# Windowed attention followed by a highway layer: x transposed by a DMA, and the set-up moved off VectorE

## The chip, the cores and the metric

The kernel runs on one core of a Trainium2 chip. The metric is the time of one execution on the device, in microseconds (us). Each kernel was run several times; a run counts as fast when it lies within 1.5% of the fastest run of the same kernel, and only fast runs are compared. Ratios are the mean time of one kernel's fast runs over that of the other kernel's fast runs of the same rounds, so they are not quite the ratio of the medians that are quoted. Spans (139.0, 159.3) are those of the one profiled execution, from its first to its last instruction, and are a little shorter than the run's time. The granted clock is the share of full speed at which the chip let TensorE run.

## The reference, cut to what matters

```python
batch, n_heads, seq, head_dim = (4, 8, 768, 64)
n_sink, window = (4, 128)
scores = scale * np.matmul(q, k.transpose(0, 1, 3, 2))
keep = is_sink | in_window          # the first 4 keys, and the last 128
a = softmax(where(keep, scores, -1e9))
attn = np.matmul(a, v)
x = attn.transpose(0, 2, 1, 3).reshape(B * S, H * D)      # 3072 x 512
H = np.maximum(x @ w_h, 0.0)
T = 1.0 / (1.0 + np.exp(-(x @ w_t + b_t)))
out = T * H + (1.0 - T) * x
```

## The kernel before

The 3072 tokens are worked through in 24 chunks of 128 tokens (six chunks per batch). One trip of the loop holds pieces of four chunks, so that the engines overlap. The two products of the highway layer contract over the 512 features of x, and the program's matmuls for them read x with its features on the partitions: x, called `xh` in the program, is transposed into `xT` between the attention of a chunk and its highway layer. What TensorE computes is then copied (evacuated) by ScalarE or VectorE into the tile that the next step reads.

```python
    def stage_T(n):                       # q and k of a chunk: transposed on TensorE
        ...
        nc.scalar.copy(out=qT, in_=tp[:, 0:NHP, :])
        nc.vector.tensor_copy(out=kT, in_=tp[:, NHP:2 * NHP, :])

    def stage_sink_setup(b):              # once per batch: the 4 sink keys and values
        for hh in range(2):
            nc.vector.tensor_copy(out=ks3[rows, :, 4 * hh:4 * hh + NSINK],
                                  in_=kT[rows, :, 0:NSINK])
        ...  # two TensorE matmuls with a selection matrix into vps, then
        for g in range(2):
            nc.vector.tensor_tensor(out=vs[:, g, :, :], in0=vps..., in1=bdm..., op=ALU.mult)

    def stage_A(n):                       # weights times v, then the division
        ...
        nc.vector.reciprocal(out=rec.unsqueeze(2), in_=avh[:, :, 64:65])
        nc.vector.tensor_tensor(out=xh, in0=avh[:, :, 0:D], in1=rec..., op=ALU.mult)

    def stage_X(n):                       # x transposed on TensorE
        for j in range(NOC):
            nc.tensor.transpose(xtp[:, j, :], xh[:, 2 * j:2 * j + 2, :], ident)
        nc.scalar.copy(out=xT, in_=xtp)

    def stage_Mt(n):                      # the gate: x @ w_t into tps, tanh
    def stage_Mh(n):                      # x @ w_h into hps, then dd, ee, otok on VectorE
        ...
        nc.sync.dma_start(out=out[n * P:(n + 1) * P, :], in_=otok)

        for i in range(-2, NB + 1):
            s = i + 1
            ...                           # sink scores of i and i+1, every second trip
            stage_S(s); stage_A(i); stage_T(i + 2)
            load(i + 2 + AHEAD); load_v(i + 2 + AHEAD)      # AHEAD = 8 chunks
            stage_mask(s); stage_Mt(i - 1); stage_X(i)
            stage_sink_setup(i // NSC)    # in the first chunk of a batch
            stage_Mh(i - 1)
```

`xT` of chunk i is made in trip i and used in trip i+1, by `stage_Mt(i)`. The loads of q, k and v are issued by GpSimd and come in pieces of 256 bytes of input (one head of one token, 64 numbers), cast to fp16 on the way; the trace records each load of 128 tokens as 1024 packets of 128 bytes. The stores are issued on the sync engine's queue.

The softmax here doesn't subtract the row's maximum and nothing guards it: scores larger than these inputs give would overflow.

Of the kernel before, what the change touches and what calls it, by code (L numbers as in the profile page):

```python
# [8 lines left out]

FP16 = mybir.dt.float16  # L10
FP32 = mybir.dt.float32
# [10 lines left out]
def kernel(  # L22
# [19 lines left out]
    P = 128  # L42
# [49 lines left out]
        nc.gpsimd.dma_start(out=vt[:, :, 0:D], in_=v[b, :, rows, :].transpose([1, 0, 2]))  # L92


    ebias = const.tile([P, 1], FP32, tag="ebias")
    nc.vector.memset(ebias, _EXP_BIAS)
    wh_sb = const.tile([P, NOC, DM], FP16, tag="wh")
    wt_sb = const.tile([P, NOC, DM], FP16, tag="wt")
    ident = const.tile([P, P], FP16, tag="ident")
    mask = const.tile([P, 2, P], FP16, tag="mask", name="mask")  # L100
    nc.vector.memset(ident, 1.0)
    nc.vector.memset(mask, 1.0)
    for vt in v_ring:
        nc.vector.memset(vt, 2.0)

    with tc.manual_schedule(engines={ENG.Pool}):
        load(0)
        nc.gpsimd.affine_select(
            out=ident, in_=ident, compare_op=ALU.is_equal, fill=0.0,
            base=0, pattern=[[-1, P]], channel_multiplier=1)  # L110
        load_v(0)
        load(1)

        nc.gpsimd.affine_select(
            out=mask[:, 1, :], in_=mask[:, 1, :], compare_op=ALU.is_ge, fill=0.0,
            base=0, pattern=[[1, P]], channel_multiplier=-1)
        load_v(1)
        nc.gpsimd.affine_select(
            out=mask[:, 0, :], in_=mask[:, 0, :], compare_op=ALU.is_ge, fill=0.0,
            base=-1, pattern=[[-1, P]], channel_multiplier=1)  # L120
        load(2)
        nc.gpsimd.dma_start(out=wt_sb, in_=moe_w_t.rearrange("(kc p) of -> p kc of", p=P))
        load_v(2)
        load(3)
        nc.gpsimd.dma_start(out=wh_sb, in_=moe_w_h.rearrange("(kc p) of -> p kc of", p=P))
        load_v(3)
        bdm = const.tile([P, H], FP32, tag="bdm")
        nc.gpsimd.memset(bdm, 1.0)
        bdm3 = bdm.rearrange("p (a b) -> p a b", b=2)
        nc.gpsimd.affine_select(  # L130
            out=bdm3, in_=bdm3, compare_op=ALU.is_ge, fill=0.0,
            base=0, pattern=[[-32, NHP], [-4, 2]], channel_multiplier=1)
        nc.gpsimd.affine_select(
            out=bdm3, in_=bdm3, compare_op=ALU.is_ge, fill=0.0,
            base=NSINK - 1, pattern=[[32, NHP], [4, 2]], channel_multiplier=-1)
        for n in range(4, AHEAD):
            load(n)
            load_v(n)

    mask0 = const.tile([P, P], FP16, tag="mask0", name="mask0")  # L140
    nc.vector.tensor_copy(out=mask0, in_=mask[:, 1, :])
    nc.vector.memset(mask0[0:NSINK, :], 1.0)
    mask1 = const.tile([P, 2, P], FP16, tag="mask1", name="mask1")
    nc.vector.tensor_copy(out=mask1, in_=mask)
    nc.vector.memset(mask1[0:NSINK, 0, :], 1.0)


    bt32 = const.tile([1, DM], FP32, tag="bt32")
# [3 lines left out]
    ones_row = const.tile([P, P], FP16, tag="ones_row")  # L152
    nc.vector.memset(ones_row, 0.0)
    nc.vector.memset(ones_row[0:1, :], 1.0)
    nc.vector.tensor_scalar_mul(bt16[0:1, :], bt32, 0.5)


    sel = const.tile([P, NHP, 32], FP16, tag="sel")
    nc.vector.memset(sel, 0.0)
    for hh in range(2):  # L160
        nc.vector.tensor_copy(
            out=sel[:, :, 4 * hh:4 * hh + NSINK],
            in_=ident[:, 0:NSINK].unsqueeze(1).to_broadcast([P, NHP, NSINK]))
    ks_bd = []
    for i in range(2):
        t = const.tile([P, NHP * 160], FP16, tag=f"ks{i}", name=f"ks{i}")
        nc.vector.memset(t, 0.0)
        ks_bd.append(t)


    qkT = {}
    e_of = {}
    es_of = {}
    vs_of = {}
    xh_of = {}
    xT_of = {}

    def stage_T(n):
        qsd, ksd = qk_sd.pop(n)
        tp = m_ps.tile([P, 2 * NHP, P], FP16, tag="m", name="tp")  # L180
        for j in range(NHP):
            nc.tensor.transpose(tp[:, j, :], qsd[:, 2 * j:2 * j + 2, :], ident)  # L182
        for j in range(NHP):
            nc.tensor.transpose(tp[:, NHP + j, :], ksd[:, 2 * j:2 * j + 2, :], ident)  # L184
        qT = qkT_pool.tile([P, NHP, P], FP16, tag="qT", name="qT")
        kT = qkT_pool.tile([P, NHP, P], FP16, tag="kT", name="kT")
        nc.scalar.copy(out=qT, in_=tp[:, 0:NHP, :])  # L187
        nc.vector.tensor_copy(out=kT, in_=tp[:, NHP:2 * NHP, :])  # L188
        qkT[n] = (qT, kT)

    def stage_sink_setup(b):

        _, kT = qkT[b * NSC]
        ks = ks_bd[b % 2]
        ks3 = ks.rearrange("p (a b) -> p a b", b=160)
        for hh in range(2):
            rows = slice(64 * hh, 64 * hh + 64)
            nc.vector.tensor_copy(out=ks3[rows, :, 4 * hh:4 * hh + NSINK],
                                  in_=kT[rows, :, 0:NSINK])
        vps = av_ps.tile([P, 2, 512], FP32, tag="av", name="vps")  # L200
        vt = v_ring[(b * NSC) % NV]
        for g in range(2):
            nc.tensor.matmul(vps[:, g, 0:260], lhsT=sel.rearrange("p a b -> p (a b)"),
                             rhs=vt[:, g * 260:(g + 1) * 260], start=True, stop=True)
        vs = es_pool.tile([P, 2, 4, 65], FP16, tag="vs", name="vs")
        for g in range(2):
            nc.vector.tensor_tensor(  # L207
                out=vs[:, g, :, :],
                in0=vps[:, g, 0:260].rearrange("p (h e) -> p h e", e=65),
                in1=bdm[:, 4 * g:4 * g + 4].unsqueeze(2).to_broadcast([P, 4, 65]),  # L210
                op=ALU.mult)
        vs_of[b] = vs

    def stage_sink(n):

# [46 lines left out]
    def stage_A(n):  # L262
        b, c = divmod(n, NSC)
        es, np_ = e_of.pop(n)
        vts = ([] if c == 0 else [v_ring[(n - 1) % NV]]) + [v_ring[n % NV]]
        av = av_ps.tile([P, 2, 4, P], FP32, tag="av", name="av")
        for g in range(2):
            first = True
            for hl in range(2):
                for hh in range(2):  # L270
                    h = 2 * (2 * g + hl) + hh
                    for pc, vt in enumerate(vts):
                        nc.tensor.matmul(  # L273
                            av[:, g, 2 * hl + hh, 0:_AVN], lhsT=es[g][:, hh, hl, pc, :],
                            rhs=vt[:, 65 * h:65 * h + _AVN], start=first,
                            stop=False, skip_group_check=True)
                        first = False
            if c >= 2:
                nc.tensor.matmul(
                    av[:, g, :, 0:65], lhsT=es_of[n][:, c % 2, :],  # L280
                    rhs=vs_of[b][:, g, :, :], start=False, stop=True,
                    skip_group_check=True)
        es_of.pop(n, None)
        avh = av.rearrange("p g h e -> p (g h) e")
        rec = r_pool.tile([P, H], FP32, tag="rec", name="rec")
        nc.vector.reciprocal(out=rec.unsqueeze(2), in_=avh[:, :, 64:65])
        xh = x_pool.tile([P, H, D], FP16, tag="xh", name="xh")
        nc.vector.tensor_tensor(  # L288
            out=xh, in0=avh[:, :, 0:D],
            in1=rec.unsqueeze(2).to_broadcast([P, H, D]), op=ALU.mult)  # L290
        xh_of[n] = xh

    def stage_X(n):
        xh = xh_of[n]
        xtp = av_ps.tile([P, NOC, P], FP16, tag="av", name="xtp")
        for j in range(NOC):
            nc.tensor.transpose(xtp[:, j, :], xh[:, 2 * j:2 * j + 2, :], ident)  # L297
        xT = x_pool.tile([P, NOC, P], FP16, tag="xT", name="xT")
        nc.scalar.copy(out=xT, in_=xtp)  # L299
        xT_of[n] = xT  # L300

    u_of = {}
# [31 lines left out]
    with tc.manual_schedule(engines={ENG.PE, ENG.DVE, ENG.Activation}):  # L334
        for i in range(-2, NB + 1):
            s = i + 1
            if 0 <= i < NB and i % NSC >= 2 and i % 2 == 0:
                stage_sink(i)
            if 0 <= s < NB:
                stage_S(s)  # L340
            if 0 <= i < NB:
                stage_A(i)
            if i + 2 < NB:
                stage_T(i + 2)
            if i + 2 + AHEAD < NB:
                load(i + 2 + AHEAD)
                load_v(i + 2 + AHEAD)
            if 0 <= s < NB:
                stage_mask(s)
            if 0 <= i - 1 < NB:  # L350
                stage_Mt(i - 1)
            if 0 <= i < NB:
                stage_X(i)
            if 0 <= i < NB and i % NSC == 0:
                stage_sink_setup(i // NSC)
            if 0 <= i - 1 < NB:
                stage_Mh(i - 1)

# [34 lines left out]
```

## Time and profile before

| | before |
|---|---|
| time, median of 4 runs | 140.74 us |
| span of the profiled run | 139.0 us |
| VectorE busy | 117.2 us, 84% |
| TensorE busy | 114.6 us, 82% |
| ScalarE busy | 90.4 us, 65% |
| last load packet | 87.0 us |

The first lines are from the page of the kernel before: busy time with its share of the span and the number of instructions, then rows of the 40 slices (each digit is the busy share of 3.5 us in tenths; PEclk is the granted TensorE clock in tenths), then the chain of waits by engine.

```profile
PE 114.6 (82%) x1312; PEld 74.1 (53%) x1312; DVE 117.2 (84%) x235; ACT 90.4 (65%) x129; POOL 66.2 (48%) x84
...
PE   0306879999999699999999699999996999999730
DVE  6895466689988999899898999898989998999590
PEclk9999999999999999999999999999999999999997
DMA  1999999999999999999999959221011021101111
...
DVE 42%; PE 33%; ACT 14%; issue 8%; DVEq 0%
```

VectorE and TensorE are both near full from slice 9 on, and the chain goes through both. The DMA row is at 9 from the second slice to the 23rd, some 80 us, and at 0 to 2 after the 25th: the loads run ahead of the compute (last load packet at 87.0 us of 139.0).

The next lines are the same kernel's groups of instructions (count, busy us, mean ns of one, idle time before, its cause). They are what the change takes away in every chunk.

```profile
L299 ACT COPY xT<-xtp 128x512 f16<-128x512 f16 x24 | 14.0, 582 | 1.4 <-PE xtp L297 0.9
L188 DVE COPY kT<-tp 128x512 f16<-128x512 f16 x24 | 10.1, 419 | 5.5 <-ACT qT L187 5.5
...
L297 PE MATMUL xtp<-ident,xh 128*128 128x128 f16 x96 | 9.7, 225 | 4.2 <-DVE xh L288 4.2
```

The timeline of the start (start us, duration, instruction, in brackets the idle time before it) shows that the first scores wait for `kT`, because VectorE is still at its constants.

```profile
7.04 0.58 ACT L187 COPY qT<-tp 128x512 f16<-128x512 f16 x1 [4.95 <-PE tp L184]
...
7.60 0.55 DVE L104 MEMSET v_101<- 128x584 f16 x1
...
10.33 0.35 DVE L188 COPY kT<-tp 128x512 f16<-128x512 f16 x1
...
10.73 0.34 PEld L242 LDWEIGHTS <-kT 64*128 64x128 f16 x8 [4.00 <-DVE kT L188]
```

Two answers for the tile `otok` give the time from the issue of a store to its landing, first for 20 to 50 us (loads running), then for 85 us to the end (loads over).

```profile
DMA to landing us min/median/max: 5.4/5.5/6.0
...
DMA to landing us min/median/max: 2.0/2.0/2.0
```

The same store takes 5.5 us beside the loads and 2.0 us alone. The last view is the table by stretches: window, length, busy time (count) of TensorE, its weight loads, VectorE, ScalarE and GpSimd, the granted clock, the DMA share and the rate.

```profile
24.00:38.00 14.00, 13.91 (x180) 9.66 (x179) 12.09 (x22) 11.25 (x17) 12.86 (x15) 1.00 2.30 177
52.00:66.00 14.00, 13.63 (x172) 9.05 (x171) 13.09 (x25) 11.28 (x17) 10.66 (x13) 1.00 2.24 185
108.00:122.00 14.00, 13.63 (x172) 9.01 (x171) 13.09 (x26) 11.31 (x16) 0.00 (x0) 1.00 0.15 57
```

TensorE is busy for 13.6 to 13.9 of each 14 us, whether loads run or not.

### The profile page before, as it was taken

To read this page: it belongs to the slowest core of one execution; us is meant where nothing else is said; L and a number is where in the kernel's file an instruction comes from. 1 tells how busy PE (TensorE), PEld (TensorE's weight loads), DVE (VectorE), ACT (ScalarE), POOL (GpSimd) and SP (SyncE) were. 2 spreads that over 40 slices of the span, in tenths; PEclk is the share of its full clock that TensorE was granted. 3 is DMA by queue.
4 is the path that set the end of the run, shared out by engine and by line. 5 is a ranking of instruction groups with operands and counts; after the bars stand their busy time and mean duration, and the time that the engine had idled before them with its cause. 6 is when DMAs were issued, how large, how long until landed. Compare 5 with 4: busy or idle time off the path is not lost.

```text
span 139.0 us, 3303 instructions
## 1 busy us (share of the span) xinstructions
PE 114.6 (82%) x1312; PEld 74.1 (53%) x1312; DVE 117.2 (84%) x235; ACT 90.4 (65%) x129; POOL 66.2 (48%) x84
## 2 busy tenths in 40 slices
PE   0306879999999699999999699999996999999730
PEld 0105656756764465667565457657652665675300
DVE  6895466689988999899898999898989998999590
ACT  3015961879775957987777497779767777873310
POOL 6999785899887987876758170000000000000000
PEclk9999999999999999999999999999999999999997
DMA  1999999999999999999999959221011021101111
GB/s 9 113 127 120 158 189 162 152 171 178 203 191 168 200 200 174 181 201 185 185 159 144 186 72 134 80 78 75 5 75 75 0 80 75 70 11 75 75 75 75
DMA packets 79408, 16.98 MB, mean 122 GB/s; under 512 B 75297, under 2 KB 76321, under 8 KB 79394
## 3 DMA queue, kind: packets, MB, share of 16 engines
q0 software_dynamic: 75936, 10.49, 112.2%
q1 hardware_dynamic: 3458, 6.30, 12.4%
q8 instruction: 10, 0.16, 0.5%
q14 instruction: 4, 0.03, 0.1%
HBM read 20.97 MB, written 6.29 MB: 196 GB/s over the span
## 4 chain that ended last, share of the span: by engine, by line
DVE 42%; PE 33%; ACT 14%; issue 8%; DVEq 0%
PE hps L321 12%; ACT e L245 9%; DVE ee L327 6%; DVE otok L330 6%; DVE e L258 6%; DVE dd L324 6%; DVE xh L288 5%; PE av L273 4%; PE tps L309 4%; DVE kT L188 4%; PE xtp L297 3%; ACT qT L187 3%; PE sps L242 3%; PE sk L222 3%; DVE vs L207 2%
## 5 line engine op out<-in xcount | busy, mean ns | idle before, releaser
L245 ACT ACTIVATE e<-sps,ebias 128x1024 f16<-128x1024 f32 (+1 forms) x48 | 47.4, 1039 | 17.5 <-PE sps L242 13.3
L309 PE MATMUL tps<-wt_sb,xT 128*128 128x512 f16 x96 | 25.5, 390 | 0.0
L321 PE MATMUL hps<-wh_sb,xT 128*128 128x512 f16 x96 | 24.6, 378 | 0.7
L84 POOL DMA_DIRECT2D qsd<-in_q_dram x24 | 21.5, 895 | 5.3 <-DMA wt_sb<-in_moe_w_t_dram 1.2
L85 POOL DMA_DIRECT2D ksd<-in_k_dram x24 | 21.4, 890 | 2.3 <-DMA wh_sb<-in_moe_w_h_dram 1.2
L273 PEld LDWEIGHTS <-e 128*128 128x128 f16 x352 | 20.4, 100 | 3.9 <-DVE vs L207 0.9
L312 ACT ACTIVATE u<-tps 128x512 f16<-128x512 f32 x24 | 14.4, 600 | 9.5 <-PE tps L309 9.5
L258 DVE TENSOR_TENSOR e<-e,mask 128x1024 f16<-128x1024 f16 x32 | 20.5, 683 | 0.0
L324 DVE SCALAR_TENSOR_TENSOR dd<-hps,xh 128x512 f16<-128x512 f32 x24 | 16.5, 688 | 3.9 <-PE hps L321 3.9
L242 PE MATMUL sps<-qT,kT 64*128 64x128 f16 x352 | 15.2, 227 | 4.6 <-DVE kT L188 3.9
L187 ACT COPY qT<-tp 128x512 f16<-128x512 f16 x24 | 14.0, 584 | 7.5 <-PE tp L184 7.5
L327 DVE SCALAR_TENSOR_TENSOR ee<-u,dd 128x512 f16<-128x512 f16 x24 | 16.6, 693 | 2.5
L288 DVE TENSOR_TENSOR xh<-av,rec 128x512 f16<-128x512 f32 x24 | 16.6, 692 | 0.8
L330 DVE SCALAR_TENSOR_TENSOR otok<-xh,ee 128x512 f32<-128x512 f16 x24 | 16.6, 692 | 0.8
L242 PEld LDWEIGHTS <-kT 64*128 64x128 f16 x352 | 10.7, 98 | 12.0 <-issue 6.8
L299 ACT COPY xT<-xtp 128x512 f16<-128x512 f16 x24 | 14.0, 582 | 1.4 <-PE xtp L297 0.9
L188 DVE COPY kT<-tp 128x512 f16<-128x512 f16 x24 | 10.1, 419 | 5.5 <-ACT qT L187 5.5
L309 PEld LDWEIGHTS <-xT 128*128 128x128 f16 x96 | 9.6, 100 | 9.1 <-issue 0.8
L182 PE MATMUL tp<-ident,qsd 128*128 128x128 f16 x96 | 10.2, 234 | 4.8 <-DMA qsd<-in_q_dram 4.8
L297 PEld LDWEIGHTS <-xh 128*128 128x128 f16 x96 | 6.3, 100 | 13.8 <-DVE xh L288 11.6
L321 PEld LDWEIGHTS <-xT 128*128 128x128 f16 x96 | 9.1, 97 | 8.2 <-issue 1.5
L297 PE MATMUL xtp<-ident,xh 128*128 128x128 f16 x96 | 9.7, 225 | 4.2 <-DVE xh L288 4.2
(84 smaller groups left out, 162.1 us busy)
## 6 DMA issues: line engine op xcount, KB each, us to landing
out_dram<-otok SPq DMA_DIRECT2D x24, 256.0 KB, 2.9
qsd<-in_q_dram POOLq DMA_DIRECT2D x24, 128.0 KB, 7.2
ksd<-in_k_dram POOLq DMA_DIRECT2D x24, 128.0 KB, 7.4
wt_sb<-in_moe_w_t_dram POOLq DMA_DIRECT2D x1, 512.0 KB, 7.9
wh_sb<-in_moe_w_h_dram POOLq DMA_DIRECT2D x1, 512.0 KB, 9.6
v_91<-in_v_dram POOLq DMA_DIRECT2D x3, 128.0 KB, 5.4
v_92<-in_v_dram POOLq DMA_DIRECT2D x3, 128.0 KB, 4.1
v_93<-in_v_dram POOLq DMA_DIRECT2D x2, 128.0 KB, 7.9
```

The lines of the kernel that those rows point to most:

```text
L84: nc.gpsimd.dma_start(out=qsd, in_=q[b, :, rows, :].transpose([1, 0, 2]))
L85: nc.gpsimd.dma_start(out=ksd, in_=k[b, :, rows, :].transpose([1, 0, 2]))
L242: nc.tensor.matmul(sps[:, hh, o:o + P], lhsT=kk[rows, hp, :], rhs=qT[rows, hp, :], start=True, stop=True)
L245: nc.scalar.activation(out=e.rearrange("p a b c d -> p a (b c d)"), in_=sps[:, :, 0:2 * np_ * P], func=AF.Exp, bias=ebias, scale=SCALE)
L258: nc.vector.tensor_tensor(out=ev, in0=ev, in1=m.unsqueeze(1).to_broadcast([P, 4, np_ * P]), op=ALU.mult)
L273: nc.tensor.matmul(av[:, g, 2 * hl + hh, 0:_AVN], lhsT=es[g][:, hh, hl, pc, :], rhs=vt[:, 65 * h:65 * h + _AVN], start=first, stop=False, ...
L288: nc.vector.tensor_tensor(out=xh, in0=avh[:, :, 0:D], in1=rec.unsqueeze(2).to_broadcast([P, H, D]), op=ALU.mult)
L309: nc.tensor.matmul(tps, lhsT=xT[:, kc, :], rhs=wt_sb[:, kc, :], start=False, stop=(kc == NOC - 1))
L321: nc.tensor.matmul(hps, lhsT=xT[:, kc, :], rhs=wh_sb[:, kc, :], start=(kc == 0), stop=(kc == NOC - 1))
L324: nc.vector.scalar_tensor_tensor(out=dd, in0=hps, scalar=0.0, in1=xh, op0=ALU.max, op1=ALU.subtract)
L327: nc.vector.scalar_tensor_tensor(out=ee, in0=u, scalar=1.0, in1=dd, op0=ALU.add, op1=ALU.mult)
L330: nc.vector.scalar_tensor_tensor(out=otok, in0=xh, scalar=2.0, in1=ee, op0=ALU.mult, op1=ALU.add)
```

## The change

It wants to take work from the two bounding engines: the four TensorE transposes of x and their ScalarE copy become one crossbar transpose (the name used here for `dma_start_transpose`, DMA_TRANSPOSE in the traces), a DMA that writes its data transposed; q and k are evacuated by one ScalarE copy, so that VectorE's `kT` copy goes; the sink set-up becomes ten small DMAs per batch on the sync engine's queue; and the start is put in order (the v buffers get two small memsets each instead of a whole one, most of them later; warm-up matmuls run on TensorE). The diff, cut to its core:

```diff
-    for vt in v_ring:
-        nc.vector.memset(vt, 2.0)
+    def init_v(vt):
+        nc.vector.memset(vt[:, 0:H * 65].rearrange("p (h e) -> p h e", e=65)[:, :, D:D + 1], 2.0)
+        nc.vector.memset(vt[:, H * 65:VW], 0.0)
+    for vt in v_ring[0:3]:
+        init_v(vt)
...  (sel, bdm and their set-up go; mask0, mask1, bt16 are filled later; eight warm-up matmuls come)
-        nc.scalar.copy(out=qT, in_=tp[:, 0:NHP, :])
-        nc.vector.tensor_copy(out=kT, in_=tp[:, NHP:2 * NHP, :])
+        nc.scalar.copy(out=qk, in_=tp)
...
     def stage_sink_setup(b):
-            nc.vector.tensor_copy(out=ks3[rows, :, 4 * hh:4 * hh + NSINK],
-                                  in_=kT[rows, :, 0:NSINK])
+            nc.sync.dma_start(out=ks3[rows, :, 4 * hh:4 * hh + NSINK],
+                              in_=kT[rows, :, 0:NSINK])
-        ...  (vps matmuls and their masked evacuation)
+        for h in range(H):
+            r = 32 * (h // 2) + 4 * (h % 2)
+            nc.sync.dma_start(out=vs_bd[b % 2][r:r + NSINK, h // 4, h % 4, :],
+                              in_=vt[0:NSINK, 65 * h:65 * h + 65])
...
     def stage_X(n):
-        xtp = av_ps.tile([P, NOC, P], FP16, tag="av", name="xtp")
-        for j in range(NOC):
-            nc.tensor.transpose(xtp[:, j, :], xh[:, 2 * j:2 * j + 2, :], ident)
-        nc.scalar.copy(out=xT, in_=xtp)
+        nc.sync.dma_start_transpose(out=xT, in_=xh.rearrange("p h d -> p (h d)"))
```

More of the change, by code (lines that the diff above doesn't have):

```diff
@@ L7 @@
 from concourse._compat import with_exitstack
-from concourse.masks import make_identity
 FP16 = mybir.dt.float16
@@ L92, in load_v @@
         nc.gpsimd.dma_start(out=vt[:, :, 0:D], in_=v[b, :, rows, :].transpose([1, 0, 2]))
+    warm = const.tile([P, DM], FP16, tag="warm")
+    nc.vector.memset(warm, 0.0)
+    ident = const.tile([P, P], FP16, tag="ident")
+    nc.vector.memset(ident, 1.0)
     ebias = const.tile([P, 1], FP32, tag="ebias")
     nc.vector.memset(ebias, _EXP_BIAS)
+    mask = const.tile([P, 2, P], FP16, tag="mask", name="mask")
+    nc.vector.memset(mask, 1.0)
+    def init_v(vt):
[3 more added lines that the diff above has]
+        init_v(vt)
     wh_sb = const.tile([P, NOC, DM], FP16, tag="wh")
     wt_sb = const.tile([P, NOC, DM], FP16, tag="wt")
-    ident = const.tile([P, P], FP16, tag="ident")
-    mask = const.tile([P, 2, P], FP16, tag="mask", name="mask")
-    nc.vector.memset(ident, 1.0)
-    nc.vector.memset(mask, 1.0)
-    for vt in v_ring:
-        nc.vector.memset(vt, 2.0)
     with tc.manual_schedule(engines={ENG.Pool}):
@@ L125 @@
         nc.gpsimd.dma_start(out=wh_sb, in_=moe_w_h.rearrange("(kc p) of -> p kc of", p=P))
-        load_v(3)
-        bdm = const.tile([P, H], FP32, tag="bdm")
-        nc.gpsimd.memset(bdm, 1.0)
-        bdm3 = bdm.rearrange("p (a b) -> p a b", b=2)
-        nc.gpsimd.affine_select(
-            out=bdm3, in_=bdm3, compare_op=ALU.is_ge, fill=0.0,
-            base=0, pattern=[[-32, NHP], [-4, 2]], channel_multiplier=1)
-        nc.gpsimd.affine_select(
-            out=bdm3, in_=bdm3, compare_op=ALU.is_ge, fill=0.0,
-            base=NSINK - 1, pattern=[[32, NHP], [4, 2]], channel_multiplier=-1)
-        for n in range(4, AHEAD):
-            load(n)
-            load_v(n)
-    mask0 = const.tile([P, P], FP16, tag="mask0", name="mask0")
-    nc.vector.tensor_copy(out=mask0, in_=mask[:, 1, :])
-    nc.vector.memset(mask0[0:NSINK, :], 1.0)
-    mask1 = const.tile([P, 2, P], FP16, tag="mask1", name="mask1")
-    nc.vector.tensor_copy(out=mask1, in_=mask)
-    nc.vector.memset(mask1[0:NSINK, 0, :], 1.0)
     bt32 = const.tile([1, DM], FP32, tag="bt32")
@@ L154 @@
     nc.vector.memset(ones_row[0:1, :], 1.0)
-    nc.vector.tensor_scalar_mul(bt16[0:1, :], bt32, 0.5)
-    sel = const.tile([P, NHP, 32], FP16, tag="sel")
-    nc.vector.memset(sel, 0.0)
-    for hh in range(2):
-        nc.vector.tensor_copy(
-            out=sel[:, :, 4 * hh:4 * hh + NSINK],
-            in_=ident[:, 0:NSINK].unsqueeze(1).to_broadcast([P, NHP, NSINK]))
-    ks_bd = []
+    mask0 = const.tile([P, P], FP16, tag="mask0", name="mask0")
+    mask1 = const.tile([P, 2, P], FP16, tag="mask1", name="mask1")
+    ks_bd, vs_bd = [], []
     for i in range(2):
@@ L168, with warm_up, late_constants @@
         ks_bd.append(t)
+        t = const.tile([P, 2, 4, 65], FP16, tag=f"vs{i}", name=f"vs{i}")
+        nc.vector.memset(t, 0.0)
+        vs_bd.append(t)
+    def warm_up(n):
+        w = m_ps.tile([P, DM], FP32, tag="m", name="wps")
+        for _ in range(n):
+            nc.tensor.matmul(w, lhsT=warm[:, 0:P], rhs=warm, start=True, stop=True)
+    def late_constants():
+        nc.vector.tensor_copy(out=mask0, in_=mask[:, 1, :])
+        nc.vector.memset(mask0[0:NSINK, :], 1.0)
+        nc.vector.tensor_copy(out=mask1, in_=mask)
+        nc.vector.memset(mask1[0:NSINK, 0, :], 1.0)
+        nc.vector.tensor_scalar_mul(bt16[0:1, :], bt32, 0.5)
     qkT = {}
@@ L173 @@
     es_of = {}
-    vs_of = {}
     xh_of = {}
@@ L184, in stage_T @@
             nc.tensor.transpose(tp[:, NHP + j, :], ksd[:, 2 * j:2 * j + 2, :], ident)
-        qT = qkT_pool.tile([P, NHP, P], FP16, tag="qT", name="qT")
-        kT = qkT_pool.tile([P, NHP, P], FP16, tag="kT", name="kT")
-        nc.scalar.copy(out=qT, in_=tp[:, 0:NHP, :])
-        nc.vector.tensor_copy(out=kT, in_=tp[:, NHP:2 * NHP, :])
+        qk = qkT_pool.tile([P, 2 * NHP, P], FP16, tag="qkT", name="qkT")
+        nc.scalar.copy(out=qk, in_=tp)
+        qT = qk[:, 0:NHP, :]
+        kT = qk[:, NHP:2 * NHP, :]
         qkT[n] = (qT, kT)
@@ L193, in stage_sink_setup @@
         _, kT = qkT[b * NSC]
-        ks = ks_bd[b % 2]
-        ks3 = ks.rearrange("p (a b) -> p a b", b=160)
+        ks3 = ks_bd[b % 2].rearrange("p (a b) -> p a b", b=160)
         for hh in range(2):
             rows = slice(64 * hh, 64 * hh + 64)
-            nc.vector.tensor_copy(out=ks3[rows, :, 4 * hh:4 * hh + NSINK],
-                                  in_=kT[rows, :, 0:NSINK])
-        vps = av_ps.tile([P, 2, 512], FP32, tag="av", name="vps")
+            nc.sync.dma_start(out=ks3[rows, :, 4 * hh:4 * hh + NSINK],
+                              in_=kT[rows, :, 0:NSINK])
         vt = v_ring[(b * NSC) % NV]
-        for g in range(2):
-            nc.tensor.matmul(vps[:, g, 0:260], lhsT=sel.rearrange("p a b -> p (a b)"),
-                             rhs=vt[:, g * 260:(g + 1) * 260], start=True, stop=True)
-        vs = es_pool.tile([P, 2, 4, 65], FP16, tag="vs", name="vs")
-        for g in range(2):
-            nc.vector.tensor_tensor(
-                out=vs[:, g, :, :],
-                in0=vps[:, g, 0:260].rearrange("p (h e) -> p h e", e=65),
-                in1=bdm[:, 4 * g:4 * g + 4].unsqueeze(2).to_broadcast([P, 4, 65]),
-                op=ALU.mult)
-        vs_of[b] = vs
+        for h in range(H):
+            r = 32 * (h // 2) + 4 * (h % 2)
+            nc.sync.dma_start(out=vs_bd[b % 2][r:r + NSINK, h // 4, h % 4, :],
+                              in_=vt[0:NSINK, 65 * h:65 * h + 65])
     def stage_sink(n):
@@ L280, in stage_A @@
                     av[:, g, :, 0:65], lhsT=es_of[n][:, c % 2, :],
-                    rhs=vs_of[b][:, g, :, :], start=False, stop=True,
+                    rhs=vs_bd[b % 2][:, g, :, :], start=False, stop=True,
                     skip_group_check=True)
@@ L342 @@
                 stage_A(i)
+            if i == -2:
+                warm_up(8)
             if i + 2 < NB:
                 stage_T(i + 2)
-            if i + 2 + AHEAD < NB:
-                load(i + 2 + AHEAD)
-                load_v(i + 2 + AHEAD)
+                if (i + 2) % NSC == 0:
+                    stage_sink_setup((i + 2) // NSC)
+            if i == -2:
+                late_constants()
+            for n in ([i + 2 + AHEAD] if i > -2 else range(3, AHEAD + 1)):
+                if n < NB:
+                    if n > 3:
+                        load(n)
+                    if 3 <= n < NV:
+                        init_v(v_ring[n])
+                    load_v(n)
             if 0 <= s < NB:
@@ L353 @@
                 stage_X(i)
-            if 0 <= i < NB and i % NSC == 0:
-                stage_sink_setup(i // NSC)
             if 0 <= i - 1 < NB:
```

## The prediction

> **What bounds it now.** In the page's busy table VectorE has 117.2 us (84%) and TensorE 114.6 (82%) of a 139.0 us span; ScalarE has 90.4. The table by stretches gives 9.3 to 10.0 us per pair of 128-token chunks, VectorE 8.0 to 9.2 of it, TensorE 8.5 to 9.6. The chain of waits says VectorE 42%, TensorE 33%, ScalarE 14%: it alternates. In odd chunks VectorE's mask, dd, ee, otok, xh, kT run back to back; after a sink the chain passes through sk, es, e, the q and k copies. So a period of about 4.85 us per chunk, with both engines near their limit.
>
> **Start.** The first scores matmul starts at 10.73 us; it waited for kT, which VectorE copies only at 10.33, after eleven 0.55 us memsets and its other constants, though k's transposes ended at 7.0.
>
> **Removed, per chunk.** VectorE: kT 0.42, set-up (0.8 for vs and 0.4 to 0.6 for ks per six chunks) about 0.2. TensorE: four xtp transposes, 0.22 to 0.40. ScalarE: qT 0.58 and xT 0.58 go, one 128x1024 copy comes, about 1.1 as the e activation of that width: even.
> Limits then: VectorE about 4.2, TensorE about 4.4 us. At best 0.4 x 23 = 9 us, plus about 3 us of start (scores at about 8 us; VectorE is free by then, and the warm-up matmuls fall in TensorE's wait for q until 4.8 us): a floor near 129.
>
> **Added.** One 128x512 crossbar transpose per chunk and ten small DMAs per batch, all on the queue that also carries the stores.
> Its slack: xT(i) is wanted about one period plus 0.4 us after A(i), and xh(i) ends about 1.2 us after A(i): 3.6 to 3.8 us. Round the loop, xh(i) -> transpose -> Mt, Mh (1.9) -> sink, S, A of i+2 (2.0) -> xh (1.1) gives period = (latency + 5.0)/2.
> Latency: stores on that queue land after 2.0 us from 86 us on, but 5.4 to 6.0 us before 50 us, with the DMA row at 9. [...] My estimate [...] 6 or more beside loads, behind a store. So about 5.3 us per chunk for the first eight to ten chunks (+4 us), 4.45 for the rest (-5).
> The set-up DMAs: an issue on this queue takes 0.33 us; ten, after a wait for the q/k copy, put the transpose of chunks 4, 10 and 16 off by about 4 us. I count 2 to 3 us each, +8.
> Sum: 140.6 - 3 + 4 - 5 + 8 = 144.6; some of the delays overlap, so 143.
>
> **What would show it.** First scores near 8 us. TensorE's longest wait: tps on the transpose, xT, mostly before 70 us; landing 5 us or more early[...]. Gaps of 2 to 4 us at chunks 4, 10, 16 with the queue issuing ks and vs. Late periods about 4.45. VectorE busy down about 17 us, its share below 75%.
>
> **What would make it wrong.** A transpose of about 2 us even beside loads, or set-up DMAs moved behind the transposes by the queue's order: then 128 to 133. A transpose that holds its queue or takes 6 us alone: 155 or more. If the transposes also slow the loads, q and k become the wait.
>
> Median 143 us, range 129 to 158; faster by over 2% 0.34, within 2% 0.16, slower 0.50.

The sum: 140.6 - 3 + 4 - 5 + 8 = 144.6 us, put at 143. Its +4 rests on a latency of 6 us beside loads, about what the stores took there (5.4 to 6.0 us), its -5 on a late period of 4.45 us, about the limit of 4.4 counted for TensorE, and its +8 on issues of 0.33 us and a wait for the q/k copy. That a transpose alone lands early enough for 4.45 us was the estimate.

## The result, and the profile after

The changed kernel is correct and took 163.56 us in the median of 4 runs (161.0 to 168.36) against 140.74 us. The ratio of the fast runs is 1.148, with a 95% interval of 1.137 to 1.158: it is slower by about 15%. Its runs scatter more than those of the kernel before; two of the four lay over 1.5% above the fastest.

The same lines of the page as before, now of the changed kernel (a slice is now 4.0 us):

```profile
PE 119.1 (75%) x1216; PEld 71.0 (45%) x1216; DVE 100.9 (63%) x206; ACT 87.8 (55%) x105; POOL 65.7 (41%) x81
...
PE   6437728991967669199699498699999879999450
DVE  7145310785376177428957538877978998799831
PEclk9965555799599789969999969999999999999965
DMA  2999999999999999999999999993333322233311
...
DMA 44%; PE 32%; ACT 10%; DVE 8%; issue 4%; POOL 1%; ACTq 0%; DVEq 0%; SPq 0%; POOLq 0%
DMA xT<-xh 37%; PE hps L307 12%; PE tps L295 9%; ACT e L234 6%; DMA ks_154<-qkT 4%; ACT qkT L184 3%; PE av L262 3%; DVE xh L277 3%; PE sps L231 3%; DMA ksd<-in_k_dram 3%; PE sk L211 3%; DVE ee L313 2%; DVE dd L310 2%; PE av L268 1%; DVE rec L275 1%
```

VectorE did lose 16.3 us of work (117.2 to 100.9), as intended. But the chain now runs through the DMA of `xT` for 37% of the span, TensorE has holes as long as the DMA row is full, and in many of these slices its granted clock falls below full. (TensorE's busy time did not fall although it has 96 matmuls fewer: those at the lower clock take longer, and the warm-up matmuls count too. The four behind the transpose of chunk 6, at 67.2 us and half clock, took 1.89 us, against 1.04 at full clock; over the run one of these took 420 ns in the mean, 390 before.)

The waits of the changed kernel (us in total, times, longest) name the tile:

```profile
DVE dd L310 <- PE hps L307: 38.8, 23, 7.5
ACT u L298 <- PE tps L295: 31.1, 15, 4.6
PEld L295 <- DMA xT<-xh: 30.1, 16, 4.0
PE tps L295 <- DMA xT<-xh: 24.4, 14, 3.6
```

TensorE waits for the transpose, and VectorE and ScalarE wait for TensorE. The timeline shows one chunk beside loads and one after them; SPq is the sync engine issuing.

```profile
45.17 0.69 DVE L277 TENSOR_TENSOR xh<-av,rec 128x512 f16<-128x512 f32 x1
45.93 1.20 SPq L285 DMA_TRANSPOSE xT<-xh  x1
...
53.05 1.59 PE L295 MATMUL tps<-wt_sb,xT 128*128 128x512 f16 x4 [2.14 <-DMA xT<-xh]
...
148.71 1.20 SPq L285 DMA_TRANSPOSE xT<-xh  x1
...
151.18 1.04 PE L295 MATMUL tps<-wt_sb,xT 128*128 128x512 f16 x4 [2.06 <-DMA xT<-xh]
```

From the issue to the matmul that uses it, the transpose at 45.93 us took 7.1 us, the one at 148.71 took 2.5. The four matmuls behind it also took 1.59 us instead of 1.04; the granted clock was at half from 53.4 to 56.8 us.

The same three stretches of the changed kernel:

```profile
24.00:38.00 14.00, 11.32 (x110) 6.91 (x110) 8.26 (x14) 7.65 (x9) 10.50 (x13) 0.80 2.46 148
52.00:66.00 14.00, 9.26 (x90) 5.00 (x90) 8.71 (x16) 7.23 (x8) 9.85 (x12) 0.88 2.22 170
108.00:122.00 14.00, 13.40 (x156) 8.55 (x155) 11.90 (x22) 10.77 (x15) 0.00 (x0) 1.00 0.30 77
```

In the first two TensorE does about half to two thirds of the instructions of before, at a clock of 0.80 and 0.88. In the third it is back at its former pace.

The trace also records every DMA packet. A transpose is 512 packets of 256 bytes, a store 128 packets of 2 KB. From these records, the end of each `xh`, the issue, and the first use by `stage_Mt` (all in us, changed kernel, fast run):

```
chunk  xh ready  to issue  issue to     first to     last packet  xh ready
                           first packet last packet  to use       to use
  2      31.84     0.03       2.71         3.03         1.62        7.38
  4      45.86     0.06       4.80         1.43         0.89        7.18
  6      59.43     0.03       4.39         2.15         1.17        7.74
  9      78.71     0.06       2.38         2.06         1.10        5.60
 13     101.73     0.03       2.78         1.72         0.76        5.29
 22     144.47     0.06       1.18         0.78         0.51        2.53
 23     148.64     0.06       1.18         0.78         0.51        2.53
```

Alone the transpose takes 2.5 us: 1.2 us before its first packet, 0.8 us of packets, 0.5 us to the use. Beside the loads, in chunks 4 to 7, most of the extra time passes before its first packet (4.4 to 5.2 us of 7.2 to 8.8); in chunks 8 to 13 (2.0 to 3.3 us before it) the longer packets and the later use are as large a part. With no loads beside it the 131 KB of one transpose took 0.78 us of packets (168 GB/s), the 262 KB of a store 0.82 us (320 GB/s). The sync engine took 1.2 us to issue a transpose (median), 0.33 us for a store and 0.6 to 0.7 us for most of the small set-up copies.

Where the 20.3 us of span (139.0 to 159.3) went can be read from the times at which `xh` is ready. The columns are the time of chunk 0, the mean period per chunk over three stages (the step from chunk 14 to 15 lies between them: 5.00 us before, 4.94 after, 8.71 in a_sink_old), the time from the last `xh` to the end, and the span. The rows below the first two belong to the experiments; all of these profiles are of fast runs.

```
kernel            chunk 0   0 to 4   4 to 14   15 to 23   last xh to end    span
before             16.2      5.49      4.87      4.76           9.1        139.0
after              14.8      7.77      6.14      4.55          10.6        159.3
a_pe_x             14.8      5.41      4.60      4.57           9.1        133.0
p_sink_old         14.1      5.77      4.84      4.72           9.0        137.3
h_hybrid           14.3      5.64      4.60      4.50           9.9        133.7
a_sink_old         14.3      7.54      6.22      4.51          10.1        161.5
a_late_mt          14.0      6.57      5.57      4.49          10.0        147.8
a_late_sink_old    14.7      6.53      4.68      4.50          10.1        138.5
a_few_loads        14.3      7.77      4.75      4.53          10.0        144.0
s_few_loads        14.6      7.99      4.68      4.48          10.0        144.6
```

Between before and after, the first four chunks lose 4 x 2.28 = 9.1 us and the next ten 10 x 1.27 = 12.7 us; the start gains 1.4 and the last eight chunks gain 8 x 0.21 = 1.7. All of the loss but 1.6 us lies in the first 14 chunks, while loads run (they end at 108.1 us after the change, at 87.0 before); the 1.6 us come after the last `xh`, where TensorE waits 2.1 us for the last transpose.

### The profile page after: what moved, and what is told of

It is laid out like the page before. It is cut to its first block, busy times and chain, and to the rows that moved or that the text cites. A ratio compares the mean times of both kernels' runs of the same rounds, so it can differ in the third digit from the quotient of the medians.

```text
span 159.3 us, 3197 instructions
## 1 busy us (share of the span) xinstructions
PE 119.1 (75%) x1216; PEld 71.0 (45%) x1216; DVE 100.9 (63%) x206; ACT 87.8 (55%) x105; POOL 65.7 (41%) x81
## 4 chain that ended last, share of the span: by engine, by line
DMA 44%; PE 32%; ACT 10%; DVE 8%; issue 4%; POOL 1%; ACTq 0%; DVEq 0%; SPq 0%; POOLq 0%
DMA xT<-xh 37%; PE hps L307 12%; PE tps L295 9%; ACT e L234 6%; DMA ks_154<-qkT 4%; ACT qkT L184 3%; PE av L262 3%; DVE xh L277 3%; PE sps L231 3%; DMA ksd<-in_k_dram 3%; PE sk L211 3%; DVE ee L313 2%; DVE dd L310 2%; PE av L268 1%; DVE rec L275 1%
## 5 line engine op out<-in xcount | busy, mean ns | idle before, releaser
L295 PE MATMUL tps<-wt_sb,xT 128*128 128x512 f16 x96 | 28.1, 420 | 24.4 <-DMA xT<-xh 24.4
L307 PE MATMUL hps<-wh_sb,xT 128*128 128x512 f16 x96 | 29.5, 437 | 2.3 <-ACT qkT L184 2.0
L184 ACT COPY qkT<-tp 128x1024 f16<-128x1024 f16 x24 | 24.3, 1014 | 9.6 <-PE tp L182 9.6
L231 PE MATMUL sps<-qkT 64*128 64x128 f16 x352 | 15.6, 233 | 3.3 <-ACT qkT L184 3.3
L231 PEld LDWEIGHTS <-qkT 64*128 64x128 f16 x352 | 11.4, 102 | 11.2 <-issue 9.3
L182 PE MATMUL tp<-ident,ksd 128*128 128x128 f16 x96 | 10.0, 230 | 1.3 <-DMA ksd<-in_k_dram 1.3
L275 DVE RECIPROCAL rec<-av 128x8 f32<-128x8 f32 x24 | 4.8, 202 | 7.3 <-PE av L262 6.3
L293 PE MATMUL tps<-bt_147,ones_row 128*128 128x512 f16 x24 | 9.4, 390 | 0.0
L214 ACT ACTIVATE es<-sk,ebias 128x256 f16<-128x256 f32 x8 | 3.8, 473 | 9.7 <-PE sk L211 9.7
```

The costliest lines, as they stand in the source:

```text
L184: nc.scalar.copy(out=qk, in_=tp)
L231: nc.tensor.matmul(sps[:, hh, o:o + P], lhsT=kk[rows, hp, :], rhs=qT[rows, hp, :], start=True, stop=True)
L295: nc.tensor.matmul(tps, lhsT=xT[:, kc, :], rhs=wt_sb[:, kc, :], start=False, stop=(kc == NOC - 1))
L307: nc.tensor.matmul(hps, lhsT=xT[:, kc, :], rhs=wh_sb[:, kc, :], start=(kc == 0), stop=(kc == NOC - 1))
```

## The experiments

The theory: the crossbar transpose has to land within one trip of the loop; beside loads it does not (7.2 to 8.8 us from `xh` to the use in chunks 4 to 7, where the prediction counted a slack of 3.6 to 3.8), and TensorE, whose matmuls the program puts in a fixed order, stands still (24.4 us of waits for `xT`). Rivals: the set-up DMAs on the same queue; the store that stands ahead of each transpose in that queue; too much work for the DMA engines altogether, so that loads come late; and TensorE's clock, which was 0.80 and 0.88 in the two stretches with waits.

### a_pe_x: x transposed on TensorE again, the rest of the change kept

```diff
-        nc.sync.dma_start_transpose(out=xT, in_=xh.rearrange("p h d -> p (h d)"))
+        ...  (stage_X of the kernel before)
```

> The changed kernel with one part undone: x is transposed on TensorE again and evacuated by ScalarE; the new start, the merged q/k copy and the set-up by small DMAs stay. Theory A (the crossbar transpose's latency is the whole loss): the loss of 22 us is gone and what is left gains over the kernel before; ScalarE gets 0.58 us a chunk more (about 4.6 us a chunk), TensorE 0.25; about 132 us, range 128 to 137. Rival B (the small set-up DMAs on the sync queue, or a slower flow of loads, cause it): 150 us or more, with waits on ks or on q and k.

Measured: 135.07 us in the median (134.67 to 136.04), ratio to before 0.963 (0.958 to 0.969). The loss is gone and the rest of the change gains 3.7%. So the crossbar transpose is the whole loss: 159.3 - 133.0 = 26.3 us of span, of which 24.9 us have been lost when `xh` of chunk 14 is ready (107.3 against 82.4 us).

### b_dma_x: the kernel before with the crossbar transpose alone

```diff
-        ...  (stage_X of the kernel before)
+        nc.sync.dma_start_transpose(out=xT, in_=xh.rearrange("p h d -> p (h d)"))
```

> The kernel before with one part of the change alone: the crossbar transpose in place of the TensorE transposes, at the same place in the program. Theory A: slower than before by 20 us or more, about 163 to 170 us, with tps waiting for xT some 25 us. Rival B (the set-up DMAs are needed for the loss): within 3% of before, 137 to 145.

Measured: 169.28 us in the median; only one of four runs was fast, at 164.01 us, 1.168 of before's fast runs. The transpose alone causes a loss of that size, with no set-up DMA in the program. In this run's trace every transpose but one was issued within 0.1 us of `xh`, and for chunks 0 to 7 it still took 7.5 to 9.3 us from `xh` to the use. (The profiled run was one of those over 1.5% above the fastest.)

### a_late_mt: the highway products one more trip behind

```diff
-        for i in range(-2, NB + 1):
+        for i in range(-2, NB + 2):
-            if 0 <= i - 1 < NB:  stage_Mt(i - 1)          # stage_Mh alike
+            if 0 <= i - 2 < NB:  stage_Mt(i - 2)
-    x_pool = ... bufs=4
+    x_pool = ... bufs=5
```

> The changed kernel with the gate and H products (Mt, Mh) two iterations behind instead of one, so that each transpose has one more period (about 4.5 us) before it is wanted, 8 us in all against the 7 to 8 us that it took. Nothing is taken from the DMA engines. Theory A (latency, not throughput): waits on xT almost gone, 128 to 136 us in spite of one more trip of the loop. Rival C (the DMA engines have too much to do, and loads or stores come late): 150 us or more, with the wait moved to q, k or the store.

Measured: 151.7 us in the median, ratio 1.080 (1.075 to 1.086). A miss between the two forecasts: of the 26.3 us of span, 11.5 are gone. The sync queue's timeline shows what remained (start, duration, what was issued):

```profile
57.02 0.64 SPq L200 DMA_DIRECT2D vs<-v  x1
57.76 1.22 SPq L285 DMA_TRANSPOSE xT<-xh  x1
59.03 4.00 SPq L200 DMA_DIRECT2D vs<-v  x6
63.12 0.39 SPq L318 DMA_DIRECT2D out_dram<-otok  x1
65.10 1.22 SPq L285 DMA_TRANSPOSE xT<-xh  x1
```

The two transposes here are of chunks 6 and 7, whose `xh` was ready at 49.98 and 57.33 us: they were issued 7.8 us late, with set-up DMAs and a store ahead of them in the queue. In the changed kernel itself such delays are rare (1.7, 2.0 and 0.9 us, at chunks 0, 3 and 11).

### a_late_sink_old: the same, and the sink set-up back on VectorE and TensorE

The diff is that of a_late_mt plus `stage_sink_setup` of the kernel before.

> Mt and Mh two iterations behind, and the sink set-up back on VectorE and TensorE. With the two-iteration lag alone (151.7 us) the trace shows transposes of chunks 3 to 8 and 12 issued 1 to 8 us after xh was there, behind set-up DMAs and stores in their queue. Theory E (what the lag left of the loss was this waiting in the queue): 134 to 143 us, issue within 0.1 us of xh. Rival (the lag left something else, such as late loads): 148 us or more.

Measured: 139.96 us in the median, ratio to before 0.992 (0.988 to 0.997). Every transpose is now issued within 0.1 us of `xh`. Their first packets still start 4.6 to 5.6 us after the issue in chunks 3 to 16, and their last ones end 6.6 to 7.7 us after it, yet the period over chunks 4 to 14 is 4.68 us, against 6.14 in the changed kernel, and the clock over 52 to 66 us is back at 1.00. The DMA row of its page, and its line of the table by stretches:

```profile
DMA  0999999999999999999999999999999633222431
...
52.00:66.00 14.00, 12.71 (x151) 8.42 (x151) 12.41 (x23) 10.62 (x13) 8.41 (x10) 1.00 2.03 172
```

So it is latency, not throughput: the DMA engines could do all this work in time. TensorE's waits for q and k came to 6.2 us in all, against 3.9 in a_pe_x; late loads are a small part at most. Yet the loads end at 108.4 us here, although the loop is as fast as the kernel before (`xh` of chunk 14 at 87.5 us, 86.8 there, where loads end at 87.0): the transposes do lengthen the loads, without any help from a slow loop. And even with one more trip of slack the crossbar gained nothing: p_sink_old below, the same program with TensorE transposes and no extra trip, took 138.12 us.

### a_sink_old: the set-up alone undone

The diff: `stage_sink_setup` of the kernel before in the changed kernel.

> The changed kernel with the sink set-up put back on VectorE and TensorE; transposes by the crossbar, new start and merged copy stay. Theory A2: within 3% of the changed kernel, 158 to 167 us. Rival B (the ten set-up DMAs per batch in front of the transposes cost the 8 us that the prediction counted): 150 to 156.

Measured: 166.0 us in the median, 163.42 us as the mean of its two fast runs, against 161.35 for the two fast runs of the changed kernel. The set-up DMAs are not the cause of the loss; taking them away gained nothing.

### a_store_act: the stores on another queue

```diff
-        nc.sync.dma_start(out=out[n * P:(n + 1) * P, :], in_=otok)
+        nc.scalar.dma_start(out=out[n * P:(n + 1) * P, :], in_=otok)   # one trip later
```

> The changed kernel with the 24 output stores issued on ScalarE's queue, one iteration later, so that no transpose stands behind a 256 KB store [...]. Theory A1 (most of the excess latency is the store ahead in the same queue: in the trace a transpose's first packet starts 3 to 5.5 us after its issue beside loads, 1.5 us alone): latency about 4.5 to 5 us, period about 4.8, 138 to 147 us. Rival A2 (the excess comes from the loads [...] whatever the queue): within 3% of the changed kernel, 157 to 168 us.

Measured: 167.98 us in the median, ratio to before 1.187 (1.179 to 1.195). The theory that the store ahead in the queue is the main cause of the wait falls. Without stores in their queue, transposes of chunks 3 to 6 still waited 3.4 to 4.8 us for their first packet. In its profile the transposes of chunks 0, 3 and 6 were issued 2.7 to 4.7 us late, behind set-up DMAs, so the total says little by itself. (Its profiled run lay over 1.5% above its fastest.)

### a_few_loads and s_few_loads: most of the loads taken away

```diff
-                if n < NB:
-                    if n > 3: load(n)
+                if n < NV:                       # v: 11 chunks, q and k: 8; wrong result on purpose
+                    if 3 < n < AHEAD: load(n)
-        qsd, ksd = qk_sd.pop(n)
+        qsd, ksd = qk_sd[n % AHEAD]
```

> Wrong result on purpose: the changed kernel, but q and k are loaded for the first 8 chunks only and v for the first 11; later chunks compute on those again. All engine work, all transposes, stores and set-up DMAs stay; two thirds of the load traffic goes, so it ends near 35 us instead of 105. Theory A2 (a transpose takes 7 to 8 us [...]; alone 2.5): from chunk 5 or so the first packet starts 1.2 us after the issue, period 4.5 us, in all 135 to 142 us. Rival D (the transpose is slow by itself or because of the stores and set-up DMAs on its own queue): 153 us or more.

Measured: 148.85 us in the median, 146.17 for its only fast run, which is the profiled one; 1.038 of before's fast runs. The total missed the forecast, but what the loads do to the transpose shows itself sharply. Its page has the DMA and clock rows

```profile
PEclk9975555899559999999999999999999999999997
DMA  1999999999982281422331315213322233113311
```

and as soon as the loads are over (last packet at 40.9 us), from chunk 4 on, the first packet comes 1.2 us after the issue in all but one chunk, and the period over chunks 4 to 14 falls from 6.14 to 4.75 us. What was left was the first four chunks (7.77 us each, as in the changed kernel) and a few transposes that were issued up to 2.5 us late behind set-up DMAs. The second run takes those out by putting the set-up back on VectorE and TensorE:

> Wrong result on purpose: q and k loaded for 8 chunks, v for 11, as in the earlier run of this kind (148.85 us), with the sink set-up back on VectorE and TensorE. That run left open why it was still 14 us above the version with TensorE transposes. Theory H (the first four chunks, while the 8 chunks and the weights are still loading, lose 9 us, and set-up DMAs ahead in the queue the rest): chunk 4 as late as before, near 44 us, then a period of about 4.55; 146 to 149 us, with issue within 0.1 us of xh. Rival (something else in the crossbar path costs after loads are over): period 4.7 or more.

Measured: 146.58 us in the median, ratio 1.040 (1.032 to 1.048). Every transpose but one was issued within 0.1 us, and after chunk 4 (46.6 us) the periods are 4.68 and 4.48 us. The remaining distance to the version with TensorE transposes is the first four chunks, while the first loads and the weights are still coming in (in a_few_loads the DMA row is at 9 to its 11th slice, 40 us).

### a_ahead4 and s_ahead4: loads four chunks ahead instead of eight

```diff
-    AHEAD = 8
+    AHEAD = 4
```

> The changed kernel with loads running 4 chunks ahead of use instead of 8 (one number; buffers and rings shrink with it). The same 256-byte pieces are loaded in all, but once the first four chunks are in, they come only as chunks are used up[...]. Theory G (a transpose waits 4 to 5 us for its first packet because a backlog of loads stands queued [...]): from chunk 4 on the wait falls to 1.5 to 3 us, the middle period from 6.1 to about 5 us, in all 143 to 153 us. Rival (any load traffic delays it as much, backlog or not; or loads now come late): within 3% of the changed kernel or slower, with waits on q and k.

Measured: 165.1 us in the median, 162.25 for its only fast run. The wait for the first packet did fall, to 1.2 to 2.8 us for chunks 4 to 13, but the time missed. Set-up DMAs, which now waited for v, held four transposes back by 1.8 to 4.8 us.

> Loads 4 chunks ahead in place of 8, and the sink set-up back on VectorE and TensorE, so that no set-up DMA that waits for a late v can hold a transpose back in the queue (with it, 4 chunks ahead took 165.1 us though the first-packet wait fell to 1.8 to 2.8 us). Theory G (the backlog of loads is what a transpose waits behind): wait 1.2 to 3 us from chunk 4 on, issue within 0.1 us of xh, middle period 5.0 to 5.5 us, in all 148 to 158 us. Rival (the backlog is not it): 162 or more.

Measured: 164.16 us in the median, ratio 1.164 (1.158 to 1.171): the time missed again. Issues were within 0.1 us in all but one chunk, the first packets came after 1.8 to 3.5 us in chunks 4 to 7 (4.4 to 5.0 us in a_sink_old, the same program with eight chunks ahead). In chunks 8 to 13 there was nothing to gain: 1.9 to 3.4 us, 1.7 to 2.8 in a_sink_old. The packet records tell why. Count the load packets (1024 a load) that had been issued and had not ended when a transpose was issued. In the changed kernel they were 4300 to 5400 in chunks 4 to 7 (wait 4.4 to 5.2 us), 1000 to 1900 in chunks 8 to 13 (2.0 to 3.3 us) and none from chunk 15 on (1.2 us); in a_late_sink_old 4100 to 5700 in chunks 3 to 16 (4.6 to 5.6 us). So a backlog of loads does lengthen the wait; but 4.5 to 7.5 us still passed from `xh` to the use in chunks 4 to 13, and with loads spread out to 130 us (108 us there) the trouble lasted for 18 chunks instead of 14. Pacing the loads gave back later what it saved early. (Both profiles are of runs over 1.5% above the fastest.)

### a_warm, a_warm6 and s_warm6: TensorE kept busy while it waits

```diff
         tps = m_ps.tile([P, DM], FP32, tag="m", name="tps")
+        for _ in range(6 if 1 < n < 14 else 0):     # a_warm: 16 for n < 8, 8 for 8 <= n < 14
+            nc.tensor.matmul(tps, lhsT=warm[:, 0:P], rhs=warm, start=True, stop=True)
```

> The changed kernel with dummy matmuls (16 for each of chunks 0 to 7, 8 for each of 8 to 13) in front of the gate product, where TensorE waits for xT: they keep it busy [...] (granted clock 0.87 now, 5 to 8 tenths in the waiting stretches) and change no DMA. Theory F (a good part of the loss is TensorE at half clock [...]): 150 to 157 us. Rival (the clock is a symptom; the loop waits for the transpose either way): within 2%, 160 to 167; more than that if the dummies themselves come in the way.

Measured: 171.75 us, ratio 1.218. The dummies overshot: `stage_Mt` came 2 to 6 us after the last packet of its transpose in chunks 2 to 9, so this run says nothing about the clock.

> As the run with dummy matmuls that overshot (171.75 us), but with 6 for chunks 2 to 13 only, 1.3 us at full clock inside waits of some 3.3 us. Theory F (TensorE at half clock [...] is a good part of the loss): 150 to 158 us, clock 0.95 or more. Rival (the loop waits for the transpose either way): 160 to 167, with the clock up all the same.

(The 1.3 us are an estimate, six times 0.22 us: four matmuls of this width took 1.04 us at full clock in the changed kernel, and a single one 0.38.)

Measured: 166.32 us, ratio 1.182. Set-up DMAs held the transposes of chunks 5 and 6 back by 5.7 and 8.5 us, which the dummies had not been meant to touch.

> Six dummy matmuls in front of the gate product of chunks 2 to 13, with the sink set-up back on VectorE and TensorE: without the held-up queue of chunks 5 and 6 that spoiled the earlier run of this kind (166.3 us). Theory F (TensorE's fallen clock is a good part of the loss): 150 to 158 us. Rival (the loop waits for the transpose either way): 162 to 169, against 166.0 without the dummies.

Here the set-up is back on VectorE and TensorE, and the issues are on time. Measured: 159.73 us in the median, ratio 1.126 (1.118 to 1.133); its fast runs average 158.42 us, against 163.42 for a_sink_old, the same program without dummies. That is between the two forecasts: the dummies saved 5.0 us although they cost time themselves. In the two profiles `stage_Mt` and `stage_Mh` together took 2.4 us in the mean of chunks 4 to 13 without dummies and 1.9 with them. I estimate from this, with the loop's period of half the time round it, that the clock accounts for some 2.5 of the 5.0 us over these ten chunks. The rest is not attributed, and the runs' mean clocks do not settle it: 0.927 and 0.928 in the fast runs with dummies, 0.934 and 0.882 without. So the fallen clock is a part of the loss, by this estimate 2.5 to 5 of the 26 us. From 24 to 38 us the two profiles stand the other way round, 0.99 without dummies and 0.81 with them. The lines of the table by stretches for 52 to 66 us, first of a_sink_old, then of s_warm6 (the clock is the third number from the end; the profile of s_warm6 is of a run over 1.5% above its fastest):

```profile
52.00:66.00 14.00, 10.50 (x92) 6.04 (x92) 9.17 (x18) 7.24 (x8) 10.48 (x12) 0.74 2.28 169
```

```profile
52.00:66.00 14.00, 10.93 (x107) 5.88 (x105) 9.65 (x21) 7.39 (x9) 9.86 (x12) 1.00 2.46 168
```

### p_sink_old and h_hybrid: what the rest of the change is worth

p_sink_old is a_pe_x with the set-up also back on VectorE and TensorE. h_hybrid is a_pe_x with the crossbar for the last nine chunks, after the loads:

```diff
+        if n < 15:
             ...  (TensorE transposes and ScalarE copy)
+        else:
+            nc.sync.dma_start_transpose(out=xT, in_=xh.rearrange("p h d -> p (h d)"))
```

> The changed kernel with x transposed on TensorE and the sink set-up back on VectorE and TensorE too: of the change only the new start and the merged q/k copy are left. Against the version with TensorE transposes and set-up by DMA (135.07): the set-up is about 1.3 us of VectorE and 0.6 us of TensorE per six chunks. If it lies on the critical path, 136.5 to 139 us; if TensorE alone bounds this version, within 0.5% of 135.

> x transposed on TensorE for chunks 0 to 14, while loads run, and by the crossbar for 15 to 23, when they are over and a transpose lands 2.5 us after xh. In the traces the late period is 4.55 us with the crossbar and 4.57 with TensorE, so the crossbar should gain nothing there: 134 to 136.5 us, within 1% of 135.07. If TensorE's freed 0.25 us a chunk counts when the latency fits, 132 to 133.

Measured: p_sink_old 138.12 us, ratio 0.982 (0.977 to 0.987); h_hybrid 135.84 us, ratio 0.965 (0.960 to 0.969). So the new start and the merged copy gain about 1.8%, and the set-up by small DMAs another 1.9% (0.963 for a_pe_x), with no transpose in their queue. The crossbar gains nothing measurable even where it lands in time: its late period is 4.50 us against 4.57. The best version is a_pe_x, faster than both kernels.

## Why the prediction was wrong

It forecast 143 us, at most 158, and the kernel took 163.56. That it came out on the slower side was luck: without the +8 us for the set-up DMAs, which did not come, its own sum is 136.6 us, faster than before.

- **What bounds the kernel, and the intended savings: right.** VectorE's busy time fell by 16.3 us (about 17 forecast) to 63% of the span (below 75%). The late period came to 4.55 us (about 4.45).
- **The start: right.** The first scores began at 7.91 us instead of 10.73 (about 8 forecast). `xh` of chunk 0 is 1.4 us and that of chunk 1 is 3.0 us earlier.
- **The loop: right in form.** Two chunks per round, period = (latency + 5.0) / 2. Over chunks 4 to 13 the mean time from `xh` to the use was 6.7 us, which gives 5.8; the measured period was 6.14. The rest fits with `stage_Mt` and `stage_Mh`, which took 2.4 us in the mean of these chunks in place of 1.9 (3.3 in the chain at 53 us, at the lower clock); half of the 0.5 us makes it 6.1.
- **The step that failed: "about 5.3 us per chunk for the first eight to ten chunks (+4 us)".** The term that was mis-sized is the latency beside loads. It was set at "6 or more" and then used as if it were 6 at the most (by the formula even 6 gives 5.5). Measured from `xh` to the use, it was 9.8 us in the mean of the first four chunks and 6.7 in the next ten; the formula then gives 7.4 and 5.8. Measured: 7.77 us per chunk for the first four and 6.14 for the next ten, together 21.8 us lost where 4 had been counted. Three things were missed. The latency was 7.2 to 8.8 us in chunks 4 to 7 and 7.4 to 12 in the first four (1.7 and 2.0 us of it, in chunks 0 and 3, were late issues). The loads lasted to 108 us instead of 87, and so 14 chunks were hit instead of 8 to 10. The transposes alone can do that (a_late_sink_old, 108.4 us at the old pace); the slower loop also holds loads back (GpSimd waits 12.3 us for `av` before loading v), and how much each adds is not shown. The prediction had named slower loads as a risk, with q and k as the wait, but TensorE waited only 3.4 us for q and k. And TensorE's clock was at half in five stretches before 108 us, 34 us in all, which cost 2.5 to 5 us more (an estimate from s_warm6). Alone the transpose took 2.5 us; what had been underestimated was its time beside loads.
- **The set-up DMAs "put the transpose of chunks 4, 10 and 16 off by about 4 us ... +8": wrong.** Those three were issued 0.06 to 0.08 us after `xh`. The queue's order had the small DMAs of these batches behind those transposes, which the prediction had named as something that would make it wrong. Each took 0.6 to 0.7 us to issue, not 0.33, and still a_sink_old was no faster without them. Where TensorE transposes x, they are even a gain of about 2%. In the changed kernel they held back chunks 0 and 3 (1.7 and 2.0 us). They hurt more only where other changes to the loop let them stand ahead of a transpose while they waited (a_late_mt, a_ahead4, a_warm6, and up to 2.5 us in a_few_loads).
- **"-5" for the late chunks: too large.** The last eight chunks gained 1.7 us: the period before was 4.76 there, not 4.85, and the loads left fewer chunks in this stage.

The runs show that the loads lengthen the transpose, and that the stores in its queue are not the main cause: with the stores on another queue the first packets still waited 3.4 to 4.8 us (a_store_act), with most loads gone 1.2 us (a_few_loads). The clock does not follow the waits as closely: it was 0.80 and 0.88 in the stretches with waits and 1.00 in the other, but of 14 waits of TensorE for `xT` only those of chunks 2, 4, 6 and 10 ended within 0.5 us of the start of a stretch at half clock, and the first of the five stretches at half clock began at 9.0 us, before any transpose was issued.

What stays open is where a transpose's packets stand while they wait 4 to 5 us beside loads. That the backlog of loads lengthens the wait is shown by both runs with loads four chunks ahead and by the counts of packets; the place of the queueing is not shown by any run. The loss in the first four chunks (9.1 us), while the weights load too, was not taken apart by a run of its own; moving the transposes alone to another queue was not tried.

## What to carry to other kernels

A DMA put in the middle of a dependent chain must be costed at the latency that DMAs show in that stage of the same kernel, and with a margin: the store already showed 5.5 us beside loads and 2.0 alone, and the transpose showed 7 to 8 and 2.5. Compare it with the slack, then either give it another trip of the loop (with the transposes issued on time, that made the middle period 4.68 us again) or leave the work where it was: the four TensorE transposes took 0.22 us each (median) beside the loads and after them. Count also what the new DMA does to the other traffic: here the loads ended 21 us later. And look at the clock behind a wait of TensorE: here the matmuls behind one took 1.59 us instead of 1.04, most of that time at half clock.
